# Groups of the last batch in the attention's last steps, and a home of its own for the second MoE's first 512 tokens

## The chip, the core and the metric

The kernel runs on one core of one Trainium2 chip. The metric is the time of one execution on the device in microseconds (us), as the median of the runs shown. An execution under the hardware profiler gave the trace that is read here.

## The reference, cut to what matters

```python
# 4 batches, 8 heads, 576 tokens, head width 64; 2304 tokens in all
q_rot, k_rot = rotate(q), rotate(k)
attn = softmax(q_rot @ k_rot.T / 8); x = (attn @ v) as [2304, 512]
# first MoE: w1, w2, w3 [512, 768], w_out [768, 512]
y = maximum(maximum(x @ w1, x @ w2), x @ w3) @ w_out
# second MoE: w_in [512, 2048], w_out [2048, 512]
h = y @ w_in
out = (h * sigmoid(h)) @ w_out
```

## The kernel before

Every product of float32 accuracy is made of three float16 matmuls on a high and a low part ("split": ScalarE rounds the high part, VectorE takes the rest).

**Attention.** `attention()` runs 80 steps, one tile of 128 query rows each, and four more to drain. A step issues the scores of one tile (`s`, L380 to L390), the maximum of a row on VectorE (`nb`, L400), the exponential on ScalarE (`e`, L407), and for the two tiles before it the division (L419), the transposes on TensorE (`tr`, L434 to L448) with their copies to SBUF (`pt`, L436 to L454), and the product with v (`xp`, L463 and L467) whose result is split into `x` (L470, L471). The attention's PSUM pools stay open until its end.

**First MoE.** `moe1(b, ...)` yields the work of a batch as groups: an "up" group is 12 matmuls on 256 or 320 tokens (`PARTS`: half 0 has 256 tokens, half 1 has 320) for one of the three weights, a "down" group 18. Three up groups make one tile `h`: the first is evacuated by ScalarE (`t`, L560), the second and third by VectorE (`t`, L562). Inside the attention a group has one of the two PSUM buffers `ps_m` (tag `m`); behind the attention `ps_g` (tag `mg`, five buffers) comes to them. In the attention's loop groups of the first three batches are let in by a rate (`RATE`, `debt`); those of the last batch, b = 3, are written behind it. The order within an engine is settled when the program is built, by a scheduler that may move an instruction ahead where its operands allow it.

**Second MoE.** `prep_w7` combines and splits its second weight on POOL (`z`, L793), ScalarE (L797) and VectorE (L801) beside the last batch's groups: eight items, a new one every 5.2 groups, with three buffers `z7`. The first MoE's result lies in DRAM (`yscr`). Nine blocks of 256 tokens follow. Block 0 goes through `s1` in four units (`yt`, L920). Blocks 1 to 8 go in four pairs J = 0 to 3 of 512 tokens through `s1_pair`, eight steps each, which replaces eight products by seven (L952); for that the 512 tokens are loaded into four blocks of a tile `yr` (L742), their largest value is taken over all rows (`y7_max`: L150 on VectorE, then a transpose L117 on TensorE, L119 on VectorE and a broadcast matmul L120), four differences are made on POOL (L987) and the seven forms are split in place (`y7_forms`, L158 and L163): form b overwrites block b from block b + 1. The activations of a unit are combined on POOL (`gsum`, L899), split (L903, L904) and multiplied by `s2` (L1014, L1016). In `s1_pair` VectorE adds the banks `m` and `mb` up (L958), and one of the sums is POOL's (`z`, L966), before ScalarE's activation (L970). `yr` has two buffers of eight blocks; they lie in the space of the first MoE's weights, so that the first load waits for that MoE's last up group. `DIFFS` gives the order of the four differences.

All loads named here go through SyncE's DMA queue (SP), in the order in which they are issued; an issue that waits holds the ones behind it.

```python
DIFFS = ((4, 0, 1), (5, 2, 4), (6, 2, 0), (7, 3, 5))   # out, in0, in1: r[out] = r[in0] - r[in1]
```

Of the kernel before, what the change touches and what calls it, by code (L numbers as in the profile page):

```python
# [17 lines left out]
P = 128  # L18
# [4 lines left out]
def fused_kernel(  # L23
# [52 lines left out]

    left = ExitStack()
    wp1 = Ring(left, "wp1", 1)
    x_p = {0: Ring(left, "x0", 1)}
# [376 lines left out]
    def av(b, hp, r):  # L456
        if hp == 0 and r == 0:
            x_t[b] = x_p[b % 2].tile([P, NP, 2, S], F16, tag="x", name="x")
# [312 lines left out]

    SUMS = ((4, 0, 2, ALU.add), (6, 1, 0, ALU.subtract), (5, 4, 1, ALU.subtract), (7, 3, 5, ALU.subtract))
    DIFFS = ((4, 0, 1), (5, 2, 4), (6, 2, 0), (7, 3, 5))
# [103 lines left out]
    def moe2(st, pools, rings, ps_a, wo_rest, w7, w8_load):  # L877
        z_p, yr_p, ga_p, sum_p, g7_p, tm_p, o_p = pools
# [15 lines left out]
        def g_split(jb, u, g):  # L894
# [3 lines left out]
            for o, x, y, op in SUMS:  # L898
                nc.gpsimd.tensor_tensor(out=q[o], in0=q[x], in1=q[y], op=op)  # L899
# [77 lines left out]
        def y7_max(r):  # L977
            m = small.tile([P, 1], F32, tag="ym", name="ym")
            absmax(m, flat(r[:, 0:4]))
            return m  # L980

        def y7_sums(J, r, m):
            s, sg, ch, co = y_scales(m, 2, st)
            for jb in (1 + 2 * J, 2 + 2 * J):
                sg_t[jb], co_t[jb] = sg, co
            for o, x, y in DIFFS:
                nc.gpsimd.tensor_tensor(out=r[:, o], in0=r[:, x], in1=r[:, y], op=ALU.subtract)  # L987
            return s, ch

        def y7_forms(J, r, s, ch, lo_hi=range(7)):  # L990
            for b in lo_hi:
                t = r[:, b].bitcast(F16)
                split(t[:, 0:512], t[:, 512:1024], r[:, b + 1], s)
            if lo_hi[-1] == 6:
                sc[J] = [r[:, b].bitcast(F16).rearrange("p (x c n) -> p x c n", x=2, c=2) for b in range(7)], ch
# [77 lines left out]
        raw = y7_load(0)  # L1073
        for n in range(UNITS):
# [11 lines left out]
        for J in range(nb // 2):  # L1086
            A, B = 1 + 2 * J, 2 + 2 * J
            more = J + 1 < nb // 2
            for p in range(HB):
# [6 lines left out]
                if p == 2 and more:  # L1096
                    sums = y7_sums(J + 1, raw, m)
                if p > 2 and more:
                    y7_forms(J + 1, raw, *sums, lo_hi=((0,), (1,), (2, 3), (4, 5), (6,))[p - 3])
# [77 lines left out]
    for j, _ in enumerate(attention(), 1):  # L1177
# [35 lines left out]
    def w8_load(k):  # L1213
        t = w8a.tile([P, 2, 2, 7, P], F16, tag="w8s", name="w8s")
        p = k % HB
        if k < HB:
            for c in range(2):
                nc.sync.dma_start(out=t[:, c, :, 0:4], in_=w8scr[:, p, c, :, 0:4])
# [64 lines left out]
```

## Time and profile before

| what | value |
|---|---|
| median of three runs | 1032.52 us (1030.5 to 1036.38) |
| the profiled execution, its own time | 1033.06 us |
| its span in the trace | 1031.3 us |
| TensorE (PE) busy | 957.4 us, 93% of the span |
| VectorE (DVE) busy | 687.4 us, 67% |
| ScalarE (ACT) busy | 617.8 us, 60% |
| GpSimd (POOL) busy | 490.3 us, 48% |
| mean granted clock of TensorE | 0.976 |

The span is what the trace covers; 1.76 us of the execution's own time lie around it. Busy time of an engine is the time in which one of its instructions ran. In a row of the timeline the numbers are start, length, engine, line, operation and operands; brackets give the idle time before it on its engine and what ended it.

### The profile page before, as it was taken

How to read it: one execution, taken by the hardware profiler on the slowest of the kernel's cores; microseconds unless marked ns; L12 is line 12 of the kernel's file. 1: busy time of each engine (PE TensorE's matmuls, PEld its weight loads, DVE VectorE, ACT ScalarE, POOL GpSimd, SP SyncE). 2: the span in 40 equal slices, each digit the busy share in tenths (PEclk: the TensorE clock that was granted, in tenths of full speed). 3: DMA queues.
4: the chain of work that ended last, by engine and by line, in shares of the span. 5: the costliest groups of instructions: out<-in, count | busy, mean ns of one | idle time of the engine just before them, and what ended most of it. 6: DMA issues, size and time to landing. Idle time of an engine off the chain costs nothing.

```text
span 1031.3 us, 19508 instructions
## 1 busy us (share of the span) xinstructions
PE 957.4 (93%) x7234; PEld 716.3 (69%) x7234; DVE 687.4 (67%) x1295; ACT 617.8 (60%) x1377; POOL 490.3 (48%) x548
## 2 busy tenths in 40 slices
PE   4776988999999999989999999998999999999997
PEld 2443665666666766666766668777888888888886
DVE  6669787765577655677576646645678866867454
ACT  3778676656757767768777744534565644644342
POOL 6835593961247601543232205536269457356164
PEclk9688999999999999999999999999999999999999
DMA  6943123512434411544444414254444343342201
GB/s 151 281 117 102 32 75 90 139 51 68 137 97 121 118 47 41 164 140 138 133 134 138 144 61 165 82 186 146 129 151 162 105 154 111 109 129 95 89 3 42
DMA packets 126063, 118.00 MB, mean 114 GB/s; under 512 B 47376, under 2 KB 109584, under 8 KB 125968
## 3 DMA queue, kind: packets, MB, share of 16 engines
q1 hardware_dynamic: 124464, 116.03, 37.6%
q8 instruction: 57, 0.93, 0.4%
q10 hardware_dynamic: 1504, 0.72, 0.3%
q14 instruction: 38, 0.31, 0.1%
HBM read 90.51 MB, written 26.21 MB: 113 GB/s over the span
## 4 chain that ended last, share of the span: by engine, by line
PE 55%; DVE 10%; POOL 7%; ACT 5%; issue 4%; DMA 4%; SPq 1%; DVEq 0%; ACTq 0%; POOLq 0%
PE m L544 15%; PE m L952 5%; PE xp L467 5%; PE tr L448 4%; PE s L390 4%; PE mb L952 4%; POOL gsum L899 4%; PE mg L544 3%; PE c L1016 3%; PE b L1016 2%; PE a L1016 2%; DVE nb L400 2%; POOL yr L987 1%; PE d L1016 1%; DMA yr<-yscr 1%
## 5 line engine op out<-in xcount | busy, mean ns | idle before, releaser
L544 PEld LDWEIGHTS <-w 128*128 128x128 f16 x1632 | 157.8, 98 | 65.3 <-issue 24.6
L544 PE MATMUL m<-x,w 128*128 128x256 f16 (+1 forms) x1336 | 189.8, 287 | 9.6 <-ACT t L560 4.2
L1016 PEld LDWEIGHTS <-g 128*128 128x128 f16 x1485 | 145.2, 98 | 19.5 <-issue 2.3
L952 PEld LDWEIGHTS <-w8s 128*128 128x128 f16 x1344 | 131.0, 98 | 20.6 <-issue 5.3
L400 DVE TENSOR_REDUCE nb<-s 128x2 f32<-128x1152 f32 (+1 forms) x80 | 98.7, 1234 | 48.4 <-PE s L390 39.1
L407 ACT ACTIVATE e<-s,nb 128x576 f32<-128x576 f32 x144 | 105.2, 736 | 41.3 <-DVE nb L400 34.8
L212 POOL TENSOR_SCALAR z<-z 128x256 uint16<-128x256 uint16 x64 | 56.6, 885 | 142.4 <-DVE z L211 128.6
L793 POOL TENSOR_TENSOR z<-z 128x128 f32<-128x128 f32 (+1 forms) x96 | 59.8, 640 | 127.6 <-DMA z<-zwo 37.3
L448 PE MATMUL tr<-ident,e 128*128 128x128 f32 x576 | 98.5, 289 | 16.8 <-ACT T L350 6.1
L419 ACT ACTIVATE e<-e,rec 128x576 f32<-128x576 f32 x144 | 104.4, 767 | 15.3 <-DVE rec L417 14.7
L448 PEld LDWEIGHTS tr<-ident,e 128*128 128x128 f32 x576 | 69.8, 147 | 52.9 <-issue 11.6
L952 PE MATMUL m<-yr,w8s 128*128 128x256 f16 x768 | 90.7, 273 | 4.2 <-DVE t L958 4.2
L467 PE MATMUL xp<-pt,vd 128*64 128x256 f32 (+1 forms) x512 | 83.6, 423 | 0.0
L452 ACT ACTIVATE pt<-tr 128x384 f32<-128x384 f32 x119 | 56.5, 485 | 44.8 <-PE tr L448 44.5
L390 PE MATMUL s<-T 64*128 64x512 f32 x256 | 80.4, 690 | 0.0
L966 POOL TENSOR_TENSOR z<-t 128x256 f32<-128x256 f32 x32 | 27.9, 873 | 94.1 <-DVE t L958 55.9
L952 PE MATMUL mb<-yr,w8s 128*128 128x256 f16 x576 | 69.4, 273 | 2.3 <-ACT yr L158 2.1
L544 PE MATMUL m<-h,wo 128*128 128x256 f16 (+1 forms) x448 | 64.4, 286 | 0.5 <-POOL wo L160 0.5
L904 DVE SCALAR_TENSOR_TENSOR g<-gsum,sg,g 128x1024 f16<-128x1024 f32 x36 | 49.1, 1373 | 22.5 <-ACT g L903 22.0
L544 PEld LDWEIGHTS <-wo 128*128 128x128 f16 x512 | 49.3, 98 | 17.8 <-issue 5.8
L903 ACT ACTIVATE g<-gsum,sg 128x1024 f16<-128x1024 f32 x36 | 40.7, 1141 | 33.2 <-POOL gsum L899 33.2
L467 PEld LDWEIGHTS xp<-pt,vd 128*64 128x64 f32 x512 | 36.7, 138 | 33.4 <-issue 16.0
(231 smaller groups left out, 1919.9 us busy)
## 6 DMA issues: line engine op xcount, KB each, us to landing
w8s<-w8scr SPq DMA_DIRECT2D x64, 448.0 KB, 4.3
z<-in_moe_w_in_dram SPq DMA_DIRECT2D x32, 256.0 KB, 3.1
z<-in_moe_w_out_dram SPq DMA_DIRECT2D x32, 256.0 KB, 3.2
w<-in_moe_w_dram SPq DMA_DIRECT2D x6, 768.0 KB, 5.7
wo<-in_moe_w_dram SPq DMA_DIRECT2D x6, 768.0 KB, 5.6
qk<-in_q_dram SPq DMA_DIRECT2D x32, 128.0 KB, 3.0
vd<-in_v_dram SPq DMA_DIRECT2D x16, 256.0 KB, 3.2
zwi<-z SPq DMA_DIRECT2D x32, 128.0 KB, 3.1
```

The costliest lines, as they stand in the source:

```text
L212: nc.gpsimd.tensor_scalar(out=q[:, :, 2], in0=q[:, :, 1], scalar1=step, scalar2=off, op0=ALU.mult, op1=ALU.add)
L390: last["s"] = nc.tensor.matmul(s[:, o:o + 512], qs[r], kt[r], start=True, stop=True).ins
L400: x = nc.vector.tensor_reduce(out=nb[:, 0:m], in_=both(s, 0, 960, 576) if m > 1 else s[:, 0:576], op=ALU.max, axis=AX.X, negate=True)
L407: x = nc.scalar.activation(out=e[:, HK[g]], in_=s[:, SK[g]], func=AF.Exp, bias=nb[:, g:g + 1], accum_out=sm[:, g:g + 1])
L419: nc.scalar.activation(out=e[:, HK[g]], in_=e[:, HK[g]], func=AF.Copy, scale=r[:, g:g + 1])
L448: nc.tensor.transpose(tr[:, i * n:(i + 1) * n], e[0:n, c * P:(c + 1) * P], ident[0:n, 0:n])
L452: nc.scalar.activation(out=to, in_=of, func=AF.Copy)
L467: nc.tensor.matmul(xp[r, 0:n], v4[:, g, c, :], pt[:, c + 5 * g, :], start=False, stop=(c == 3))
L544: nc.tensor.matmul(ps[:, 0:n], l, r, start=(first and i == 0), stop=(not more and i == len(passes) - 1))
L793: nc.gpsimd.tensor_tensor(out=z[:, o], in0=z[:, x], in1=z[:, y], op=op)
L952: nc.tensor.matmul(o, l, r, start=(i == 0), stop=(i == len(passes) - 1))
L1016: x = nc.tensor.matmul(ps, l, r, start=first, stop=last_, skip_group_check=True)
```

## The change

1. In the attention's last eight steps one group of the last batch's first half is taken per step.
2. The tile of `x_p[0]` (9,216 bytes in a row; the `x` of batches 0 and 2) is allocated outside the first MoE's pools and kept. Even pairs J = 0 and 2 load their four blocks of 512 tokens there (`y7_even`); the four differences go into a tile `ye` of its own. Odd pairs keep `yr`, which now has one buffer.
3. Pair 0 is loaded at group 14 of the last batch's rest, behind the first four loads of `w8s`, and measured at group 15; the measure stood in `s1`'s second unit before. Its differences and first two forms stand ahead of `s1`, the other forms in its first two units.
4. The differences of the later pairs are held behind the last `gsum` that is written before them (`issue_after`). `DIFFS` has its second and third entries exchanged.
5. `prep_w7` starts an item every 4.4 groups, and block 0 is measured at group 9 of the rest in place of 12.

```diff
+    x_p = {0: Ring(ctx, "x0", 1)}
     left = ExitStack()
     wp1 = Ring(left, "wp1", 1)
-    x_p = {0: Ring(left, "x0", 1)}
...
+    def y7_even(J):
+        r = x_p[0].tile([P, NP * S], F32, tag="x", name="x")
+        return y_load(1 + 2 * J, r[:, 0:4 * 512].rearrange("p (a n) -> p a n", a=4), 512), None
+
+    def y7_block(r, o):
+        return r[o // 4][:, o % 4]
...
-    DIFFS = ((4, 0, 1), (5, 2, 4), (6, 2, 0), (7, 3, 5))
+    DIFFS = ((4, 0, 1), (6, 2, 0), (5, 2, 4), (7, 3, 5))
...
+                last["gsum"] = nc.gpsimd.tensor_tensor(out=q[o], in0=q[x], in1=q[y], op=op).ins
...
         def y7_load(J):
-            return y_load(1 + 2 * J, yr_p.tile([P, 8, 512], F32, tag="yr", name="yr"), 512)
...
+            if J % 2 == 0:
+                return y7_even(J)
+            r = yr_p.tile([P, 8, 512], F32, tag="yr", name="yr")
+            return y_load(1 + 2 * J, r[:, 0:4], 512), r[:, 4:8]
...
+            r = r[0], r[1] if J % 2 else ye_p.tile([P, 4, 512], F32, tag="ye", name="ye")
+            with tc.issue_after(last["gsum"]) if J else nullcontext():
+                for o, x, y in DIFFS:
+                    nc.gpsimd.tensor_tensor(out=y7_block(r, o), in0=y7_block(r, x), in1=y7_block(r, y), op=ALU.subtract)
+            return r, s, ch
...
-        raw = y7_load(0)
+        sums = y7_sums(0, st["y7"], st["y7s"])
+        y7_forms(0, *sums, lo_hi=(0, 1))
         for n in range(UNITS):
             s1(n)
             splits()
             rest_step(5)
-            if n == 1:
-                m = y7_max(raw)
+            if n < 2:
+                y7_forms(0, *sums, lo_hi=((2, 3), (4, 5, 6))[n])
             if n == 2:
                 second(0, 0)
-                y7_forms(0, raw, *y7_sums(0, raw, m))
...
+        if nxt[0] == B - 1 and j > len(tiles) - 4 and nxt[1] == 0:
+            nxt = next(moe)
...
-    chain = prep_w7(z7_p, w7_p, w7, 5.2)
+    chain = prep_w7(z7_p, w7_p, w7, 4.4)
...
-        if n == 12:
+        if n == 9:
             st["y0"] = y_split(y0, yt_p, st)
+        if n == 14:
+            with tc.issue_after(last["early"]):
+                st["y7"] = y7_even(0)
+        if n == 15:
+            st["y7s"] = y_scales(y7_max(st["y7"]), 2, st)
```

**How the order moves on TensorE, at the attention's last tile.** A row with `m` or `mg` is one matmul of the first MoE's last batch (12 make a group), `tr` are the attention's transposes, `xp` its product with v. Before:

```order
L448 MATMUL tr_6990<-ident_78,e_6892 128x128 x3
L434 MATMUL tr_6995<-ident_78,e_6923 128x128 x4
L439 MATMUL tr_7002<-ident_78,e_6923 128x128
L440 MATMUL tr_7002<-ident_78,e_6923 64x128
L463 MATMUL xp_7007<-pt_6931,vd_0_129 128x320
L467 MATMUL xp_7007<-pt_6931,vd_0_129 64x320 x8
L544 LDWEIGHTS w_0_138
L544 MATMUL mg_7107<-x_5774,w_0_138 128x256
```

Nothing stands between the last transposes and the last product. The same place in the change, with the repeats of a group's matmuls left out:

```order
L448 MATMUL tr_7053<-ident_78,e_6922 128x128 x3
L544 LDWEIGHTS w_0_138
L544 MATMUL m_7190<-x_5774,w_0_138 128x256
...
L544 MATMUL m_7304<-x_5774,w_0_138 128x256
...
L434 MATMUL tr_7073<-ident_78,e_6971 128x128 x4
L439 MATMUL tr_7080<-ident_78,e_6971 128x128
L440 MATMUL tr_7080<-ident_78,e_6971 64x128
...
L544 MATMUL m_7328<-x_5774,w_0_138 128x256
...
L463 MATMUL xp_7103<-pt_6979,vd_0_129 128x320
L467 MATMUL xp_7103<-pt_6979,vd_0_129 64x320 x8
```

Three groups now lie around the last transposes. From the first group of the last batch to the last `xp` there were 4 groups, and there are 11.

**On POOL, at the second MoE's start.** `yr_7974` is pair 0, `yr_8446` pair 1, the numbers of `gsum` are block 0's units. Before:

```order
L987 TENSOR_TENSOR yr_7974<-yr_7974 128x512 x4
L899 TENSOR_TENSOR gsum_8038<-ga_7979 128x256 x2
L987 TENSOR_TENSOR yr_8446<-yr_8446 128x512 x2
L899 TENSOR_TENSOR gsum_8107<-ga_8048 128x256
L899 TENSOR_TENSOR gsum_8038<-gsum_8038,ga_7979 128x256
L899 TENSOR_TENSOR gsum_8107<-ga_8048 128x256
L987 TENSOR_TENSOR yr_8446<-yr_8446 128x512
```

Eight differences stand among the first units' sums. In the change (`x_7514` is pair 0's new home):

```order
L1003 TENSOR_TENSOR ye_8002<-x_7514 128x512 x2
L1003 TENSOR_TENSOR ye_8002<-x_7514,ye_8002 128x512 x2
L915 TENSOR_TENSOR gsum_8070<-ga_8011 128x256 x2
L915 TENSOR_TENSOR gsum_8070<-gsum_8070,ga_8011 128x256
L915 TENSOR_TENSOR gsum_8070<-ga_8011,gsum_8070 128x256
L915 TENSOR_TENSOR gsum_8144<-ga_8085 128x256 x2
```

Only pair 0's four are left there, ahead of all sums; pair 1's have gone behind the sums of block 1's first unit.

**On POOL, where pair 0's steps end and pair 1's begin.** `yr_9273` is pair 2, `z_2` the sum of L966. Before:

```order
L899 TENSOR_TENSOR gsum_9320<-gsum_9320,z_1_8782 128x256
L987 TENSOR_TENSOR yr_9273<-yr_9273 128x512
L899 TENSOR_TENSOR gsum_9320<-z_1_8782,gsum_9320 128x256
L987 TENSOR_TENSOR yr_9273<-yr_9273 128x512
L899 TENSOR_TENSOR gsum_9200<-z_0_8384 128x256 x2
L987 TENSOR_TENSOR yr_9273<-yr_9273 128x512
L899 TENSOR_TENSOR gsum_9200<-gsum_9200,z_0_8384 128x256
L966 TENSOR_TENSOR z_2_9211<-t_1_9261 128x2x128
L987 TENSOR_TENSOR yr_9273<-yr_9273 128x512
```

Three differences stand ahead of `z_2`. In the change:

```order
L915 TENSOR_TENSOR gsum_9203<-gsum_9203,z_0_8387 128x256
L915 TENSOR_TENSOR gsum_9203<-z_0_8387,gsum_9203 128x256
L982 TENSOR_TENSOR z_2_9214<-t_1_9264 128x2x128
L915 TENSOR_TENSOR gsum_9456<-z_1_8785 128x256 x2
L915 TENSOR_TENSOR gsum_9456<-gsum_9456,z_1_8785 128x256
L1049 TENSOR_TENSOR ob_9335<-t_0_9336 128x256
L915 TENSOR_TENSOR gsum_9456<-z_1_8785,gsum_9456 128x256
L1003 TENSOR_TENSOR ye_9548<-x_9276 128x512 x2
```

All four stand behind `z_2` and two units' sums. The same exchange is found between pairs 1 and 2.

## Rows read from the trace of the kernel before

**Rows 1.** The page, part 1: busy time, share of the span, instructions.
```profile
PE 957.4 (93%) x7234; PEld 716.3 (69%) x7234; DVE 687.4 (67%) x1295; ACT 617.8 (60%) x1377; POOL 490.3 (48%) x548
```
**Rows 2.** Busy time by stretch: PE, PEld, DVE, ACT, POOL; granted clock, DMA share, GB/s.
```profile
582.79:613.77 30.98, 28.36 (x175) 17.15 (x175) 15.08 (x40) 19.57 (x51) 1.79 (x4) 0.94 0.20 65
613.77:680.87 67.10, 65.93 (x533) 51.98 (x532) 41.08 (x64) 28.47 (x48) 29.70 (x32) 1.00 0.35 111
680.87:720.00 39.13, 35.64 (x318) 30.63 (x316) 19.45 (x25) 18.36 (x23) 25.85 (x24) 1.00 0.67 219
775.00:810.00 35.00, 32.67 (x296) 28.47 (x294) 27.97 (x46) 17.70 (x27) 26.58 (x26) 1.00 0.40 130
860.00:885.00 25.00, 22.50 (x204) 19.58 (x202) 16.44 (x33) 12.23 (x19) 16.27 (x19) 1.00 0.41 122
```
**Rows 3.** PE's waits from 582.79 to 613.77: total us, times, longest.
```profile
PE xp L463 <- DVE pt L442: 1.0, 1, 1.0
PE tr L448 <- ACT pt L452: 0.7, 2, 0.5
PE tr L434 <- ACT e L419: 0.6, 1, 0.6
PE tr L448 <- DVE pt L442: 0.4, 1, 0.4
```
**Rows 4.** PE's timeline, two products of 16 matmuls; PE busy and granted clock between.
```profile
572.56 2.37 PE L467 MATMUL xp<-pt,vd 128*64 128x320 f32 x16
610.03 3.81 PE L467 MATMUL xp<-pt,vd 128*64 128x320 f32 x16
...
611.00:612.00 1.00, 1.00 (x6) 0.50 0.00 0
```
**Rows 5.** PE's timeline, a run of up groups; PE's waits in the whole program.
```profile
619.57 6.17 PE L544 MATMUL mg<-x,w 128*128 128x256 f16 x55
...
PE m L544 <- DVE t L562: 6.7, 6, 1.9
PE m L544 <- ACT t L560: 4.2, 2, 3.1
```
**Rows 6.** PE's waits from 560 to 780, those behind the attention.
```profile
PE mb L952 <- ACT yr L158: 2.1, 1, 2.1
PE m L120 <- DVE amax L119: 1.2, 1, 1.2
...
PE m L920 <- DMA w8s<-w8scr: 0.9, 1, 0.9
```
**Rows 7.** Timeline of SP's DMA queue.
```profile
619.04 20.90 SPq L850 DMA_DIRECT2D z<-zwo  x10
...
681.29 1.46 SPq L742 DMA_DIRECT2D yr<-yscr  x3
...
686.64 6.26 SPq L1218 DMA_DIRECT2D w8s<-w8scr  x8
```
**Rows 8.** POOL's timeline, pair 0's first difference; all L987, ns min/median/max.
```profile
686.60 1.27 POOL L987 TENSOR_TENSOR yr<-yr 128x512 f32<-128x512 f32 x1 [21.57 <-DMA yr<-yscr]
...
L987 POOL TENSOR_TENSOR yr<-yr x16: 1251/1268/2082, 686.6 to 862.2; 128x512 f32<-128x512 f32 x16
```
**Rows 9.** Timelines of POOL, ACT and PE where pair 1 begins.
```profile
786.73 1.27 POOL L987 TENSOR_TENSOR yr<-yr 128x512 f32<-128x512 f32 x1
...
789.58 0.72 ACT L970 ACTIVATE z<-z,ch 128x512 f32<-128x512 f32 x1 [1.97 <-POOL z L966]
...
796.72 2.78 PE L952 MATMUL m<-yr,w8s 128*128 128x256 f16 x24 [1.41 <-DVE t L958]
```
**Rows 10.** Timelines of POOL, ACT and PE where pair 2 begins.
```profile
854.13 2.50 POOL L987 TENSOR_TENSOR yr<-yr 128x512 f32<-128x512 f32 x2 [4.58 <-DMA yr<-yscr]
...
864.80 0.72 ACT L970 ACTIVATE z<-z,ch 128x512 f32<-128x512 f32 x1 [3.91 <-POOL z L966]
...
873.52 2.78 PE L952 MATMUL m<-yr,w8s 128*128 128x256 f16 x24 [2.23 <-DVE t L958]
```

More of the change, by code (lines that the diff above doesn't have):

```diff
@@ L770, in y_split, with y7_max, y7_form @@
         return yt, sg, ch, co
+    def y7_even(J):
+        r = x_p[0].tile([P, NP * S], F32, tag="x", name="x")
+        return y_load(1 + 2 * J, r[:, 0:4 * 512].rearrange("p (a n) -> p a n", a=4), 512), None
+    def y7_max(r):
+        m = small.tile([P, 1], F32, tag="ym", name="ym")
+        absmax(m, flat(r[0]))
+        return m
+    def y7_block(r, o):
+        return r[o // 4][:, o % 4]
+    def y7_form(r, b, s):
+        t = y7_block(r, b).bitcast(F16)
+        split(t[:, 0:512], t[:, 512:1024], y7_block(r, b + 1), s)
     SUMS = ((4, 0, 2, ALU.add), (6, 1, 0, ALU.subtract), (5, 4, 1, ALU.subtract), (7, 3, 5, ALU.subtract))
-    DIFFS = ((4, 0, 1), (5, 2, 4), (6, 2, 0), (7, 3, 5))
+    DIFFS = ((4, 0, 1), (6, 2, 0), (5, 2, 4), (7, 3, 5))
     HB = NF2 // 2
@@ L877, in moe2 @@
     def moe2(st, pools, rings, ps_a, wo_rest, w7, w8_load):
-        z_p, yr_p, ga_p, sum_p, g7_p, tm_p, o_p = pools
+        z_p, yr_p, ye_p, ga_p, sum_p, g7_p, tm_p, o_p = pools
         co_t, g7, acc, sc, gB, gA, ready = {0: st["y0"][3]}, {}, {}, {}, {}, {}, {}
@@ L974, in y7_load, with y7_sums @@
         def y7_load(J):
-            return y_load(1 + 2 * J, yr_p.tile([P, 8, 512], F32, tag="yr", name="yr"), 512)
[L977 to L983, printed above, removed]
+            if J % 2 == 0:
+                return y7_even(J)
+            r = yr_p.tile([P, 8, 512], F32, tag="yr", name="yr")
+            return y_load(1 + 2 * J, r[:, 0:4], 512), r[:, 4:8]
+        def y7_sums(J, r, scales):
+            s, sg, ch, co = scales
             for jb in (1 + 2 * J, 2 + 2 * J):
                 sg_t[jb], co_t[jb] = sg, co
-            for o, x, y in DIFFS:
-                nc.gpsimd.tensor_tensor(out=r[:, o], in0=r[:, x], in1=r[:, y], op=ALU.subtract)
-            return s, ch
+            r = r[0], r[1] if J % 2 else ye_p.tile([P, 4, 512], F32, tag="ye", name="ye")
[3 more added lines that the diff above has]
+            return r, s, ch
         def y7_forms(J, r, s, ch, lo_hi=range(7)):
             for b in lo_hi:
-                t = r[:, b].bitcast(F16)
-                split(t[:, 0:512], t[:, 512:1024], r[:, b + 1], s)
+                y7_form(r, b, s)
             if lo_hi[-1] == 6:
-                sc[J] = [r[:, b].bitcast(F16).rearrange("p (x c n) -> p x c n", x=2, c=2) for b in range(7)], ch
+                sc[J] = [y7_block(r, b).bitcast(F16).rearrange("p (x c n) -> p x c n", x=2, c=2) for b in range(7)], ch
         def s2(jb, u):
@@ L1096, in moe2 @@
                 if p == 2 and more:
-                    sums = y7_sums(J + 1, raw, m)
+                    sums = y7_sums(J + 1, raw, y_scales(m, 2, st))
                 if p > 2 and more:
-                    y7_forms(J + 1, raw, *sums, lo_hi=((0,), (1,), (2, 3), (4, 5), (6,))[p - 3])
+                    y7_forms(J + 1, *sums, lo_hi=((0,), (1,), (2, 3), (4, 5), (6,))[p - 3])
                 if p == 5:
@@ L1217, in w8_load @@
             for c in range(2):
-                nc.sync.dma_start(out=t[:, c, :, 0:4], in_=w8scr[:, p, c, :, 0:4])
+                last["early"] = nc.sync.dma_start(out=t[:, c, :, 0:4], in_=w8scr[:, p, c, :, 0:4]).ins
         else:
@@ L1236, in fused_kernel @@
         Ring(ctx, nm, bufs)
-        for nm, bufs in (("yr_p", 2), ("ga_p", 3), ("sum_p", 2), ("g7_p", 3), ("tm_p", 2), ("o_p", 1))
+        for nm, bufs in (("yr_p", 1), ("ye_p", 1), ("ga_p", 3), ("sum_p", 2), ("g7_p", 3), ("tm_p", 2), ("o_p", 1))
     )
```

3 lines of the change are left out of this document (1 added, 2 removed).

## The prediction

> **What bounds the kernel now.** I read the page's table of engines first, then the busy time by stretch, then the waits in each stretch that the change touches, and last the timelines around the longest waits. The table shows TensorE busy for 93% of the span [rows 1], and no other engine above 67%, so a microsecond is to be had where TensorE stands still or runs slowly, and nowhere else. The stretches show where that is [rows 2]: busy time taken from length gives 30.98 - 28.36 = 2.62 us of idle time in the attention's last steps, 67.10 - 65.93 = 1.17 in the rest of the last batch, 39.13 - 35.64 = 3.49 at the second MoE's start, 35.00 - 32.67 = 2.33 where pair 1 begins and 25.00 - 22.50 = 2.50 where pair 2 begins. That is 12.1 us. To it comes a stretch at half clock: the same 16 matmuls of `xp` took 2.37 us at 572 and 3.81 at 610, where the granted clock was 0.50, which is the level of 1.2 GHz; TensorE had just stood waiting for the attention's last copies [rows 3, 4]. That is 1.44 us more. Everything that the change moves lies in these five places, and the matmuls themselves stay as they are, so about 13.6 us bound the gain from above.
>
> **Part 1, the groups in the attention's last steps.** By the order of the instructions TensorE now has 11 groups ahead of the attention's last `xp` where it had 4, so seven groups move ahead. A group of 12 costs 12 x 6.17 / 55 = 1.35 us [rows 5], seven cost 9.4 us, and they cost it in either place. What they bring is cover. Each of the waits at 582 to 614 is for a copy or a division that the attention's own chain is late with [rows 3], and at most of these places the new order has a group or more between the transpose and the matmul that waited. I take 2.2 of the 2.62 us. The clock fell behind those waits, and with TensorE busy through them I take all of the clock's loss, 1.4 us; if a gap stays, it is 0. The unknown is what seven more groups do to the two buffers `m`: a group can't start before the one two places ahead of it has been evacuated, and its evacuation stands in the queues of ScalarE and VectorE among the attention's exponentials and maxima. The nearest rows are the waits for such evacuations in the whole program, eight of them, 10.9 us together, the longest 3.1 us [rows 5]. So the bounds are a gain of 2.62 and, with the longest of these waits at every one of the seven, a loss of 21.7; the order places the evacuations close behind their groups, so I stay near the upper end, and the 0.4 us that I left out stand for the buffers. VectorE and ScalarE are busy for 15.1 and 19.6 of these 31 us [rows 2], so they have room.
>
> What is late next: the attention ends 9.4 - 2.2 - 1.4 = 5.8 us later, and with it the loads of `w8s`, of `yscr` and of `z`, which wait for its space. The rest of the last batch starts later by the same and is 9.4 us shorter, so from the attention's end to the second MoE there are 67.1 - 9.4 = 57.7 us. POOL's 29.7, ScalarE's 28.5 and VectorE's 41.1 us of work in that stretch [rows 2] fit, though VectorE also gets pair 0's maximum and first forms. The step of 4.4 in place of 5.2 groups makes `prep_w7` end 7 x 0.8 = 5.6 groups sooner, some 7.6 us, which is about what the shorter stretch asks for. I cost it at nothing; its cover is the idle time of POOL ahead of the second MoE, 21.57 us [rows 8].
>
> **Part 2, the measure of block 0 and of pair 0.** Before, TensorE waited 1.17 us for `amax` of block 0 [rows 6]; VectorE had been held up by a split of `w7` whose load was late. In the new order this `amax` stands ahead of those splits, and 24 matmuls on 320 tokens lie between its transpose and its broadcast. A second measure, pair 0's, comes into this stretch. At its old place it cost TensorE no wait, and 33 matmuls lie around it now. Bounds: both wait as the one did (a loss of 1.2) or neither (a gain of 1.17). I take 0.8.
>
> **Part 3, pair 0 at the second MoE's start.** Its loads stood behind the last stores of the first MoE in the queue (681.29), and ahead of the next `w8s` (686.64) [rows 7]; POOL idled until they came [rows 8]; then its eight differences of 1.27 us shared POOL with the units' sums, and the forms came so late that TensorE waited 2.1 us for ScalarE's, after 0.9 us for `w8s` [rows 6]. Now the four loads go out right behind the first two tiles of `z` (619.04, 5.3 us behind the attention's end), in a stretch in which SP spends 20.90 us on ten issues, most of it waiting for buffers [rows 7], and need no space of the first MoE's weights. The differences wait only for the last up group's space and run in POOL's idle time, 4 x 1.27 = 5.1 of 21.57 us. Two of the forms stand ahead of the first activation on ScalarE: if the differences were late, they would hold it, but the idle time is four times their length. On SP the next `w8s` have four loads ahead of them in place of eight. I take 2.7 of the 3.49 us; the bounds are 0 (the forms are late again) and 3.49.
>
> **Part 4, the differences of later pairs.** Where pair 1 begins, POOL ran three differences of pair 2 ahead of `z`; ScalarE, which works in order, waited 1.97 us for `z` and only then split the next `gsum`, VectorE's additions came behind that, and TensorE waited 1.41 us for a bank [rows 9]. Where pair 2 begins it is the same with pair 3: ScalarE waited 3.91, TensorE 2.23 us [rows 10]. The new order puts all of the differences behind `z` and the sums in question. Three of them are 3.8 us, more than either wait, so these 3.64 us should go. The remaining 4.83 - 3.64 = 1.19 us hang on VectorE's maximum of 2,048 columns and on `amax`, which stay. I take 3.4. Pair 1's differences (5.1 us) now stand ahead of `z` at about 740, a new place. The bounds are the whole 4.83, and a loss of 2.23, the longest wait of this kind, should it come back there.
>
> **A rule that speaks against part 4.** A difference took 1,268 ns in the median and 2,082 at most [rows 8]. The Trainium skill, SBUF: State Buffer, "Who interferes with whom", says that a VectorE instruction with two SBUF inputs and a GpSimd instruction that reads SBUF hold each other up entirely. The spread of these durations agrees with it. By that rule moved differences are dear wherever VectorE adds and splits; this is the second rival below.
>
> **The sum.** 2.2 + 1.4 + 0.8 + 2.7 + 3.4 = 10.5 us. The profiled execution took 1033.06 us, which gives 1022.6; it stood 0.5 us above the median of 1032.52, so I forecast a median of 1022.5 us, a gain of 1.0%. A difference of 0.5%, here 5.2 us, is about what a measurement of this kernel can tell from none, so faster means below 1027.4 and slower above 1037.7.
>
> **The rivals.**
> - *The wait moves to the second MoE.* The attention ends 5.8 us later, and what begins there (loads of `z`, POOL's `prep_w7`, pair 0's differences behind it, the forms) comes late in a stretch shortened to 57.7 us. Against it: POOL's 21.57 us of idle time. For it: before, POOL worked in three bursts with gaps for loads, so that not its busy time but the round of three buffers may set the end, which a smaller step can't shorten. Then parts 2 and 3 bring nothing: 1022.5 + 0.8 + 2.7 = 1026.0 us. Chance 0.15.
> - *POOL's differences cost the same at their new places.* If each took its longest time, 2.08 for 1.27 us, beside VectorE's additions, the twelve that are moved behind sums would take 9.7 us more of POOL, and a wait of the old kind would come up behind them. Part 4 then brings nothing (1025.9), and with one new wait of 2.23 us at pair 1's differences 1028.1. Chance 0.13.
> - *The two buffers `m` hold the attention up* (slower). In the last eight steps each group must be evacuated in time by an engine that works in order through the attention. If each of the seven waits w, the gain is 10.5 - 7w: nothing at 1.5 us each, a loss of over 0.5% from 2.2 us each, which lies below the longest wait of 3.1 us [rows 5]; at 3.1 us the time is 1022.5 + 21.7 = 1044.2 us. For it: the groups come closer together than anywhere earlier in the attention. Against it: the eight waits of the whole program come to 10.9 us, 1.4 us each, and VectorE is idle for half of that stretch. Chance 0.05.
>
> **How the numbers follow.** The forecast has the rest, 0.67. Its own range goes from all of the idle and slow time gone, 1033.06 - 13.55 - 0.5 = 1019.0, to two thirds of the sum, 1025.5. The first two rivals reach 1028.1. With the run to run spread of the median the range is 1018.5 to 1028.5; the third rival and the tails stay outside, some 0.12. Faster: nearly all of the forecast's 0.67, 0.10 of the first rival's and 0.05 of the second's, 0.81. Same: the rest of those two and a little of the other, 0.14. Slower: 0.05.
>
> **What would show it.** Part 1: the four waits for `pt` and `e` [rows 3] gone, the granted clock at 1.00 at the last `xp`, whose 16 matmuls take 2.4 us, and no new waits of L544 for `t`. Part 2: no wait of L120. Part 3: `ye` computed ahead of the first `gsum`, and no wait of L952 for a form or of L920 for `w8s`. Part 4: no wait of L952 for `t` where pairs 1 and 2 begin, and none new at 740. The prediction is wrong if TensorE's idle time from 582 to 885 stays above 7 us, or if the granted clock falls at another place that the groups have left behind.

## The result, and the profile after

| | before | changed |
|---|---|---|
| median | 1031.08 us (five runs, 1030.5 to 1036.38) | 1020.71 us (five runs, 1020.31 to 1023.01) |
| ratio | | 0.9886, 95% interval 0.9862 to 0.991 |
| profiled execution, span | 1033.06, 1031.3 us | 1020.64, 1018.9 us |

The change is faster by 1.1%, and the measured time lies 1.8 us under the forecast of 1022.5 us and inside its range. Two more runs of the kernel before stand beside the three that the forecast started from, hence its other median. The page of the changed kernel, its table of engines:

```profile
PE 954.2 (94%) x7234; PEld 717.2 (70%) x7234; DVE 689.7 (68%) x1295; ACT 617.6 (61%) x1377; POOL 494.7 (49%) x548
```

Against [rows 1] the share of TensorE grew by one point, because the span shrank: its work is the same. So the time must have come out of its idle and slow stretches. To see that cleanly, equal work is compared: from the product `xp` of the attention's fourth tile from the end to the end of the last matmul. What stands ahead of it is the same in all kernels of this study, instruction by instruction on TensorE, VectorE, ScalarE and POOL. The stretch holds 3,841 matmul records in each, and I split it at the second MoE's first matmul. The busy time by stretch of the kernel before (columns: stretch, length, busy time of PE and its records, granted clock, DMA share, GB/s):

```profile
571.92:680.87 108.95, 105.14 (x781) 0.98 0.32 102
680.87:1025.94 345.07, 336.75 (x3062) 1.00 0.37 119
571.92:1025.94 454.02, 441.89 (x3841) 1.00 0.36 115
```

The same of the changed kernel:

```profile
571.73:673.93 102.20, 102.20 (x784) 1.00 0.37 119
673.93:1013.62 339.69, 336.62 (x3059) 0.99 0.37 118
571.73:1013.62 441.89, 438.82 (x3841) 1.00 0.37 118
```

The stretch is 12.13 us shorter, which is the difference of the two spans (12.4) but for 0.3 us. Of it 6.75 us come from ahead of the second MoE (three small matmuls of pair 0's measure now stand there too) and 5.38 from the second MoE. Idle time fell from 12.13 to 3.07 us (that the gain in length is 12.13 us too is chance). Busy time fell by 3.07 us as well, though the work is the same; the last section says why. What is left stands in one place. By tens of microseconds:

```profile
770.00:780.00 10.00, 9.67 (x90) 1.00 0.29 96
780.00:790.00 10.00, 9.91 (x92) 1.00 0.50 154
790.00:800.00 10.00, 7.35 (x51) 0.83 0.22 81
800.00:810.00 10.00, 10.00 (x95) 1.00 0.28 92
```

All windows from 560 to 770 and from 800 to 1010 read 10.00 at a clock of 1.00. The waits of TensorE from 575 us on are these two (total, times, longest):

```profile
PE m L117 <- DVE t L974: 2.6, 1, 2.6
PE m L968 <- DVE t L974: 0.3, 1, 0.3
```

None of [rows 3] is left, and of [rows 6] neither the form, nor `amax`, nor `w8s`. The waits of [rows 9, 10] are gone where pair 2 begins; where pair 1 begins a longer one has come. (Lines moved: L952 is now L968, L958 is L974, L966 is L982, L987 is L1003, L904 is L920.) Its chain reads so in the timeline (start, length, engine, line, operands, count, idle time before it and what ended it):

```profile
780.88 3.71 POOL L1003 TENSOR_TENSOR ye<-x 128x512 f32<-128x512 f32 x2
784.56 1.25 POOL L1003 TENSOR_TENSOR ye<-x,ye 128x512 f32<-128x512 f32 x1
785.78 0.72 POOL L982 TENSOR_TENSOR z<-t 128x256 f32<-128x256 f32 x1
...
787.84 1.26 POOL L1003 TENSOR_TENSOR ye<-x,ye 128x512 f32<-128x512 f32 x1
...
780.26 1.74 DVE L920 SCALAR_TENSOR_TENSOR g<-gsum,sg,g 128x1024 f16<-128x1024 f32 x1
...
788.11 1.80 DVE L920 SCALAR_TENSOR_TENSOR g<-z,sg,g 128x768 f16<-128x768 f32 x1 [3.99 <-ACT g L919]
789.84 1.74 DVE L920 SCALAR_TENSOR_TENSOR g<-gsum,sg,g 128x1024 f16<-128x1024 f32 x1
...
783.83 0.72 ACT L986 ACTIVATE ga<-ga,ch 128x512 f32<-128x512 f32 x1 [4.33 <-DVE ga L974]
786.53 0.72 ACT L986 ACTIVATE z<-z,ch 128x512 f32<-128x512 f32 x1 [1.98 <-POOL z L982]
...
789.16 1.04 PE L1031 MATMUL a<-w,g 128*128 128x256 f16 x8
792.85 0.27 PE L117 MATMUL m<-ident,ym 128*1 128x128 f32 x1 [2.65 <-DVE t L974]
792.96 0.81 PE L1031 MATMUL a<-w,g 128*128 128x256 f16 x4
793.56 2.77 PE L1031 MATMUL c<-w,g 128*128 128x256 f16 x12
```

It is the chain of [rows 9, 10] one step further on: three differences of pair 2 stand on POOL ahead of a step's `z`, ScalarE waits 1.98 us for that `z` and only then does the splits behind it, VectorE stands idle for 3.99 us, and its additions, which give the banks `m` back, end late. The next matmul that needs a bank happens to be the measure's transpose, L117. Behind the stop 12 matmuls of `c` take 2.77 us, at half clock; at the full clock 12 take 1.47.

### The profile page after: what moved, and what is told of

Its sections match the earlier page's. It is cut to its first block, busy times and chain, and to the rows that moved or that the text cites. A ratio compares the mean times of both kernels' runs of the same rounds, so it can differ in the third digit from the quotient of the medians.

```text
span 1018.9 us, 19509 instructions
## 1 busy us (share of the span) xinstructions
PE 954.2 (94%) x7234; PEld 717.2 (70%) x7234; DVE 689.7 (68%) x1295; ACT 617.6 (61%) x1377; POOL 494.7 (49%) x548
## 4 chain that ended last, share of the span: by engine, by line
PE 67%; DVE 8%; ACT 4%; POOL 3%; issue 2%; DMA 1%; SPq 0%; DVEq 0%; ACTq 0%; POOLq 0%
PE m L544 16%; PE m L968 7%; PE mb L968 6%; PE xp L467 5%; PE tr L448 4%; PE mg L544 4%; PE s L390 4%; PE c L1031 4%; PE a L1031 4%; PE b L1031 4%; PE d L1031 2%; DVE nb L400 2%; POOL gsum L915 1%; PE mb L936 1%; PE m L936 1%
## 5 line engine op out<-in xcount | busy, mean ns | idle before, releaser
L544 PE MATMUL m<-x,w 128*128 128x256 f16 (+1 forms) x1388 | 195.6, 286 | 9.8 <-ACT t L560 4.0
L544 PEld LDWEIGHTS <-w 128*128 128x128 f16 x1632 | 157.7, 98 | 65.3 <-issue 24.1
L968 PEld LDWEIGHTS <-w8s 128*128 128x128 f16 x1344 | 131.1, 98 | 16.1 <-issue 0.9
L407 ACT ACTIVATE e<-s,nb 128x576 f32<-128x576 f32 x144 | 105.4, 737 | 42.5 <-DVE nb L400 35.9
L982 POOL TENSOR_TENSOR z<-t 128x256 f32<-128x256 f32 x32 | 27.0, 845 | 89.1 <-DVE t L974 54.0
L544 PE MATMUL m<-h,wo 128*128 128x256 f16 (+1 forms) x448 | 64.4, 286 | 0.5 <-POOL wo L160 0.5
L920 DVE SCALAR_TENSOR_TENSOR g<-gsum,sg,g 128x1024 f16<-128x1024 f32 x36 | 49.1, 1372 | 22.0 <-ACT g L919 21.6
L544 PEld LDWEIGHTS <-wo 128*128 128x128 f16 x512 | 49.3, 98 | 17.8 <-issue 5.8
L330 POOL TENSOR_TENSOR w<-qk,sin_sb 128x384 f32<-128x384 f32 (+1 forms) x44 | 45.5, 1054 | 26.2 <-DMA qk<-in_q_dram 17.9
L562 DVE SCALAR_TENSOR_TENSOR t<-m,t 128x256 f32<-128x256 f32 (+1 forms) x82 | 37.0, 451 | 20.0 <-PE m L544 16.2
```

What stands on the lines that cost most here:

```text
L407: x = nc.scalar.activation(out=e[:, HK[g]], in_=s[:, SK[g]], func=AF.Exp, bias=nb[:, g:g + 1], accum_out=sm[:, g:g + 1])
L544: nc.tensor.matmul(ps[:, 0:n], l, r, start=(first and i == 0), stop=(not more and i == len(passes) - 1))
L968: nc.tensor.matmul(o, l, r, start=(i == 0), stop=(i == len(passes) - 1))
```

## The experiments

In the table are all kernels: where the equal stretch begins in the trace, its length, TensorE's busy and idle time in it, the number of its stops (idle times of 0.01 us or more), how often in it the granted clock fell to 0.50, and the ratio of the runs to those of the kernel before that were taken with them, with its interval.

| kernel | begins | length | busy | idle | stops | falls | median | ratio |
|---|---|---|---|---|---|---|---|---|
| before | 571.92 | 454.02 | 441.89 | 12.13 | 17 | 1 | 1031.08 | |
| the change | 571.73 | 441.89 | 438.82 | 3.07 | 3 | 1 | 1020.71 | 0.9886 (0.9862 to 0.991) |
| groups alone | 572.72 | 447.36 | 440.29 | 7.07 | 10 | 1 | 1026.97 | 0.995 (0.993 to 0.997) |
| without the groups | 570.43 | 448.32 | 442.20 | 6.12 | 10 | 2 | 1026.33 | 0.9941 (0.992 to 0.9962) |
| without the rule for differences | 574.19 | 446.09 | 439.36 | 6.73 | 6 | 1 | 1024.48 | 0.9929 (0.9904 to 0.9954) |
| differences behind z | 570.99 | 437.87 | 437.16 | 0.71 | 3 | 0 | 1017.84 | 0.9868 (0.9838 to 0.9899) |
| the change again | 570.60 | 442.42 | 439.08 | 3.34 | 4 | 1 | 1020.99 | 0.9882 (0.9851 to 0.9912) |
| differences behind z again | 571.78 | 437.88 | 437.15 | 0.73 | 3 | 0 | 1018.16 | 0.9852 (0.9826 to 0.9878) |
| rule for pair 1 alone | 573.44 | 441.05 | 437.47 | 3.58 | 5 | 0 | 1022.02 | 0.9891 (0.9868 to 0.9914) |
| four groups | 571.15 | 446.45 | 440.45 | 6.00 | 11 | 1 | 1025.48 | 0.9924 (0.9899 to 0.995) |
| early load, late measure | 569.44 | 442.20 | 437.76 | 4.44 | 5 | 0 | 1020.98 | 0.9895 (0.9874 to 0.9916) |
| late load | 571.07 | 445.88 | 439.34 | 6.54 | 7 | 1 | 1024.16 | 0.9919 (0.9896 to 0.9941) |

No edit changes the instructions ahead of the stretch, yet it begins anywhere between 569.44 and 574.19 us. So nearly 5 us of the spread between these executions arise ahead of what is studied here, and where a few microseconds are to be told apart, the length of the stretch says more than the median.

**Groups alone.** The kernel before, with

```diff
+        if nxt[0] == B - 1 and j > len(tiles) - 4 and nxt[1] == 0:
+            nxt = next(moe)
-    chain = prep_w7(z7_p, w7_p, w7, 5.2)
+    chain = prep_w7(z7_p, w7_p, w7, 4.4)
-        if n == 12:
+        if n == 9:
```

> The kernel before with the eight groups alone (the step of 4.4 and block 0's measure at its new place go with them; pair 0 stays as it was). Theory: the attention's last steps bring about 6.0 us by themselves, as in the trace of the change, and block 0's measure some 0.7, so 1024.4 us (ratio 0.9935), with the last 16 matmuls of xp at 2.4 us and TensorE busy throughout 583 to 616. By the prediction's sum, 3.6 + 0.8: 1026.7 us (0.9957). Rival, the wait moves to the second MoE's start: TensorE's idle time there grows from 3.5 to over 7 us because pair 0 is now late by what the attention's end is late, and 1028.5 us or more comes out (0.9975).

The stretch became 454.02 - 447.36 = 6.66 us shorter, the theory's size, with no stop left ahead of the second MoE. Ahead of it 7.19 us were gained; behind it 0.53 were lost again. The interval of the ratio holds both sums and leaves out the rival's 0.9975. At the second MoE's start the waits stayed:

```profile
PE mb L952 <- ACT yr L158: 2.1, 1, 2.1
...
PE m L920 <- DMA w8s<-w8scr: 0.4, 1, 0.4
```

They are no longer than before, where they were 2.1 and 0.9 us. So the attention may end later by the groups' time without the next stage waiting longer for it. The 0.53 us come from the clock, which fell behind the wait of 2.1 us here (0.83 from 710 to 720 us) and hadn't in the kernel before; shorter waits in the second MoE, 7.07 us for 8.32, give the rest back.

**Without the groups.** The change, with the first edit above undone, the step at 5.2 and the measures at groups 17, 22 and 23.

> The change without the eight groups (step 5.2 again, the measures at the same distance from the last batch's end). Theory: parts 2, 3 and 4 bring what the change's trace shows behind the attention, 0.7 + 5.0 + 0.4 = 6.1 us, so 1025.0 us (ratio 0.9941); the attention's last steps idle for 2.6 us and the last xp runs at half clock as before. By the prediction's sum, 0.8 + 2.7 + 3.4 = 6.9: 1024.2 us (0.9933), with no wait where pairs 1 and 2 begin. Rival, pair 0's early load pays only because the groups made room: 1028 us or more, with over 2 us of waits at the second MoE's start.

5.70 us: near the theory's 6.1. The second MoE's start has no wait, with or without the groups, so pair 0's home pays by itself. The two halves add up to 6.66 + 5.70 = 12.36 us against 12.13 together, but that is in part luck: their idle times fell by 5.06 and 6.01 us, 11.07 in all, against 9.06 together, and one more fall of the clock (near 800 us, besides the old one near 607) takes about as much back.

**Without the rule for the differences.**

```diff
-            with tc.issue_after(last["gsum"]) if J else nullcontext():
+            if True:
```

> The change without the rule that puts the later pairs' differences behind the sums. Theory: that rule removed one wait and made another of the same length (2.65 us and a slow clock where pair 1 begins), so its net is 0.4 us: 1021.1 us (1.000 of the change), with the waits where pairs begin at other places but 2 to 5 us in all. By the prediction's sum it is worth 3.4 us: 1024.1 us (1.0033 of the change). Rival, the rule itself costs: 1018 us or less.

The stretch grew by 4.20 us. My theory's 1.000 is wrong, and the prediction's price of 3.4 us looks right, but not for its reason. The largest wait is a new one, in the second MoE's first units:

```profile
681.97 1.27 POOL L1003 TENSOR_TENSOR yr<-yr 128x512 f32<-128x512 f32 x1 [1.61 <-DMA yr<-yscr]
...
684.87 2.95 POOL L1003 TENSOR_TENSOR yr<-yr 128x512 f32<-128x512 f32 x2
687.79 2.57 POOL L915 TENSOR_TENSOR gsum<-ga 128x256 f32<-128x256 f32 x2
690.32 1.27 POOL L1003 TENSOR_TENSOR yr<-yr 128x512 f32<-128x512 f32 x1
...
695.97 1.15 ACT L919 ACTIVATE g<-gsum,sg 128x1024 f16<-128x1024 f32 x1 [2.50 <-POOL gsum L915]
...
697.17 0.28 PE L1029 MATMUL b<-w,g 128*128 128x256 f16 x1 [3.15 <-ACT g L919]
```

Without the rule the scheduler puts pair 1's differences (`yr`) ahead of and between the first sums of block 0, since nothing else holds them there; the sums come late, ScalarE's split too, and TensorE stops for 3.15 us. This run therefore mixes two places, and the run with the rule for pair 1 alone takes them apart.

**The differences behind z.** TensorE's order stays the same, and on POOL the later pairs' differences move behind the `z` of the pair's third step. On VectorE and ScalarE a few instructions change places with a neighbour, none of them from 741 to 799 us, where the wait stood:

```diff
-            nc.gpsimd.tensor_tensor(out=place(gb, 0), ...)
+            last["z"] = nc.gpsimd.tensor_tensor(out=place(gb, 0), ...).ins
-            with tc.issue_after(last["gsum"]) if J else nullcontext():
+            with tc.issue_after(last["z"]) if J else nullcontext():
```

> The change with the later pairs' differences put behind POOL's z of the pair's third step instead of behind the last gsum; TensorE's order is the same, POOL's alone moves. Theory: the wait of 2.65 us where pair 1 begins comes from three differences (5.0 us) that stand ahead of z on POOL; behind z they hold nobody, the wait and the slow clock behind it go, 2.65 + 1.3 us: 1016.8 us (0.9962 of the change), TensorE busy for over 9.9 of every 10 us from 770 to 1000. Rival 1, differences cost the same wherever they stand, since they and VectorE's splits hold each other up: a wait of 2 us or more comes up at the next z or the next forms, 1020.7 us. Rival 2, the wait is the measure's, which takes a bank m between two groups: the same wait of 2.6 us stays at the same place, 1020.7 us.

As the theory said: 4.02 us less than the change, and 0.71 us of idle time in 437.87. The same place in its timeline:

```profile
782.56 0.77 POOL L982 TENSOR_TENSOR z<-t 128x256 f32<-128x256 f32 x1 [2.35 <-DVE t L974]
...
789.76 0.78 POOL L982 TENSOR_TENSOR z<-t 128x256 f32<-128x256 f32 x1 [2.35 <-DVE t L974]
790.50 2.49 POOL L1003 TENSOR_TENSOR ye<-x 128x512 f32<-128x512 f32 x2
792.95 3.34 POOL L1003 TENSOR_TENSOR ye<-x,ye 128x512 f32<-128x512 f32 x2
...
788.45 1.04 PE L1031 MATMUL a<-w,g 128*128 128x256 f16 x8
789.76 0.27 PE L117 MATMUL m<-ident,ym 128*1 128x128 f32 x1 [0.27 <-DVE t L974]
...
790.30 1.47 PE L1031 MATMUL c<-w,g 128*128 128x256 f16 x12
```

`z` now runs as soon as VectorE has made its operand, the differences fill the time to the next `z` at 799.51, and nobody waits for them. Both rivals fall: the measure's transpose stands where it stood and waits 0.27 us, and the differences, 5.83 us for four, are no cheaper than before, but hold nobody.

**The change and this version on one chip.** Both kernels unchanged, in the next two runs.

> The change as it is, beside the next three on one chip. Both theories: a ratio of 0.9886 to the kernel before, and in its profile 0.3 + 2.65 us of idle time between 770 and 800 with a slow clock behind it.

> The differences behind z once more, on the chip of the change. Theory (they hold nobody there): 4.0 us under the change, ratio to before 0.985, TensorE's idle time from the attention's last steps to the end 0.7 us. Rival (the gap between them on two chips was chance): the same time as the change.

The stretch is 442.42 - 437.88 = 4.54 us shorter, the median 2.83 us. The two intervals of the ratios (0.9851 to 0.9912, 0.9826 to 0.9878) overlap, but both carry the spread of the kernel before. Directly, ten of the change's eleven runs took 1019.8 us or more, and ten of this version's eleven 1019.59 or less; the traces agree, in both pairs. At 1.3% and 1.5% under the kernel before, this is the best version of the study.

**The rule for pair 1 alone.**

```diff
-            with tc.issue_after(last["gsum"]) if J else nullcontext():
+            with tc.issue_after(last["gsum"]) if J == 1 else nullcontext():
```

> The change with the rule kept for pair 1's differences alone; those of pairs 2 and 3 go back to where they were before, ahead of z and between the sums. It tells the two things apart that the run without the rule mixed. Theory: at pairs 2 and 3 the rule removed 3.6 us of idle time and brought 3.1 with a slow clock of 1.2, so without it there nothing is gained or lost: 1020.0 us (1.000 of the change; 0.9880 to before), with the old waits of 0.6, 1.4, 0.4 and 0.9 us where pairs 1 and 2 begin and none at 695 us. By the prediction's sum, 3.4 us of loss, all of it at pairs 2 and 3: 1024 us. Rival, the waits at 695 us had another cause than the order of pair 1's differences: they stay, 1024 us too but with 3 us idle at 695.

The old waits are back, the one where pair 2 begins with 0.93 us for the 2.23 of before, and the new one at 695 us is not:

```profile
PE m L968 <- DVE t L974: 2.9, 3, 1.4
PE m L117 <- DVE t L974: 0.6, 2, 0.4
```

The stretch is 441.05 us, 0.84 us shorter than the change's and 1.37 shorter than its second run's. So at pairs 2 and 3 the rule brought nothing in these executions; with it there are 3.07 us of idle time and a slow clock, without it 3.58 and none. The median of 1022.02 us lies between the 1020.0 and the 1024 that were expected and decides nothing. Even without the rule the five waits are 1.25 us shorter than before; whether the exchange in `DIFFS` or the new homes did that was not taken apart. The 446.09 - 441.05 = 5.04 us that it is worth lie at pair 1's differences, where the kernel before had no loss to remove.

**Four groups** in place of eight, with the measures and the step moved in proportion:

```diff
-        if nxt[0] == B - 1 and j > len(tiles) - 4 and nxt[1] == 0:
+        if nxt[0] == B - 1 and j > len(tiles) and nxt[1] == 0:
```

> The change with four groups let into the attention's last steps in place of eight (step 4.8 and the measures at the same distance from the last batch's end). Theory: each wait of the last steps is covered by the group that stands at its place, so those whose place is filled go and the others stay; the longest, 0.97 us ahead of the last xp, and the half clock behind it go with the last groups: 1 to 2 us over the change, 1022 us. Rival, cover is needed only at the end and eight are no better than four: the same time as the change. Rival 2, the two buffers m were a price that eight pay and four don't: under the change by up to 1 us.

4.56 us over the change, two to four times what I expected. Two of the five waits are gone, those of 0.23 and 0.58 us ahead of the last transposes, where two more groups stand now. Those of 0.46, 0.37 and 0.97 us stay, at places without a group, and two came, ahead of the first group that moved: 0.18 us for a weight's maximum (L120) and 0.36 for an exponential (L407). That leaves 2.35 us of 2.62, and `amax` of block 0 costs 0.50 us again. The half clock at the last `xp` is gone:

```profile
594.05 0.38 PE L120 MATMUL m<-amax,ones 1*128 1x1 f32 x2 [0.18 <-DVE amax L119]
594.78 0.49 PE L387 MATMUL s<-kd,T 128*128 128x128 f32 x2 [0.36 <-ACT e L407]
...
604.72 1.80 PE L544 MATMUL m<-x,w 128*128 128x256 f16 x15
...
607.02 1.47 PE L544 MATMUL m<-x,w 128*128 128x256 f16 x12
...
610.12 0.81 PE L463 MATMUL xp<-pt,vd 128*128 128x320 f32 x2 [0.97 <-DVE pt L442]
610.86 2.37 PE L467 MATMUL xp<-pt,vd 128*64 128x320 f32 x16
```

The stop of 0.97 us ahead of it is the same as in [rows 3]; in that kernel the clock fell behind it, here not. That cover works place by place holds. That the wait of 0.97 us goes with the last groups does not: it stayed. The two new waits do not come from the groups, as far as the trace shows: ScalarE stood idle for 1.95 us, up to 588.36, until a load of `z` for a weight of the second MoE had landed, and what stands behind it on ScalarE and VectorE came late. In the kernel before and in the change the same split had no idle time ahead of it; in the run without the groups it had 1.30 us. The two waits and the price of two stops are about 1 of the 4.56 us. The price on the buffers `m` doesn't show.

**Pair 0 loaded early, measured late.** The change, with measure, differences and forms where they were before:

```diff
-        if n == 15:
-            st["y7s"] = y_scales(y7_max(st["y7"]), 2, st)
...
+            if n == 1:
+                m = y7_max(st["y7"])
             if n == 2:
                 second(0, 0)
+                y7_forms(0, *y7_sums(0, st["y7"], y_scales(m, 2, st)))
```

> The change with pair 0 loaded early as now, but measured, its differences and forms put back into the second MoE's first three units as before. Theory A, the load was what came late: with it early TensorE waits for neither a form nor w8s, and the time is the change's, 1020.9 us (ratio to before 0.988). Theory B, what came late were the measure and the eleven splits and differences behind it, which stand among the units' sums: the wait for the forms stays, 1.5 to 2.5 us at some 712 us, perhaps with a slow clock, so 1023.5 us (0.9908).

442.20 us, the change's length within 0.3, as theory A says, and no wait for a form comes back. But there are two stops more, of 0.64 and 0.52 us at 729 and 736, and the one at 774 is 0.2 us longer; with what a stop costs besides (last section) that is 1.8 us, which the clock pays back here, since it stayed up behind the stop that ends at 792.5. So, by subtraction, the early load is most of part 3, and the early measure some 1.8 us of it.

**Pair 0 loaded late.** The change, with the load behind the first MoE's last store and the measure at once behind it:

```diff
-        if n == 14:
-            with tc.issue_after(last["early"]):
-                st["y7"] = y7_even(0)
...
+        with tc.issue_after(last["ys"]):
+            st["y7"] = y7_even(0)
+        st["y7s"] = y_scales(y7_max(st["y7"]), 2, st)
```

> The change with pair 0 in its home of its own, but loaded only behind the first MoE's last store, where its loads stood before, and measured at once. Theory A: the late load brings the old loss back, 0.9 us for w8s behind the four loads and 2 us for the forms, with five stops in place of none, 4.0 us in all: 1025 us (ratio to before 0.9922). Rival: four loads are half of the eight of before and the home frees POOL of the wait for the space, so that only 1 to 1.5 us comes back, 1022.2 us (0.9895). In both the measure's amax at 680 us, now late, costs a wait of up to 1.2 us more.

3.99 us over the change: theory A's size, though spread otherwise than it said. The two longest of the waits that came to those of the change:

```profile
PE m L936 <- DMA w8s<-w8scr: 2.4, 1, 2.4
PE b L1031 <- ACT g L919: 0.7, 1, 0.7
```

No wait for a form: four differences behind four loads are made in time. The late measure costs 0.25 us (L936 waits for pair 0's scale at 692). The scheduler moved TensorE's work too: the third unit's matmuls stand ahead of half of the second's, and so want their `w8s` sooner, 9.1 us behind the second MoE's first matmul in place of 10.5 in the change:

```profile
675.65 2.18 SPq L742 DMA_DIRECT2D x<-yscr  x4
...
678.66 1.92 SPq L1238 DMA_DIRECT2D w8s<-w8scr  x4
...
681.42 0.39 PE L1031 MATMUL b<-w,g 128*128 128x256 f16 x2 [0.66 <-ACT g L919]
684.17 0.82 PE L936 MATMUL m<-yt,w8s 128*128 128x256 f16 x3 [2.36 <-DMA w8s<-w8scr]
```

The second MoE's first matmul starts at 672.74 here. The first of these `w8s` is issued 5.9 us behind it and lands 11.4 us behind it; in the change, without the four loads ahead of it, these are 5.2 and 8.1 us. So the load comes 3.3 us later, 0.7 from its issue and 2.6 on its way. Had it landed as in the change, there would be no wait in this order either; had TensorE kept the change's order, the wait would be 11.4 - 10.5 = 0.9 us (an estimate), which is theory A's price for `w8s`. The other 1.4 us come from the order of the units. The clock fell behind this wait and not, as in the change, behind the one near 795 us, so it cost no more than there.

## Why the prediction was right, step by step

The sum was 10.5 us, the trace gives 12.4 between the spans and 12.1 in the stretch, the medians 10.4. Two of its terms were too small and one too large, so that the total comes near is luck in part: parts 1 to 3 gave some 4.5 us more than their 7.1, part 4 some 2.9 less than its 3.4. From the sum to the forecast there is a slip as well: 1032.52 - 10.5 is 1022.0, not 1022.5.

In what follows a stop is priced at 0.22 us beside its idle time and a fall of the clock at 1.7 us; both are estimates from the table, worked out in the last section.

**Part 1 and part 2: 3.6 + 0.8 = 4.4 us predicted, 6.75 found, and some 7.0 without the three matmuls of pair 0's measure that came here.** The mechanism is right: all waits of [rows 3] are gone, the 16 matmuls of the last `xp` take 2.37 us as [rows 4] had them at full clock, no new wait of L544 for `t` has come, and of `amax`'s 1.17 us nothing is left (0.29 in the change's second run). The mis-sized terms are the 2.2 us of idle time (the trace: all 2.62), the 0.8 (all 1.17) and the clock's 1.4. The clock had slowed the two matmuls L463 ahead of the 16 as well, 1.01 us for 0.70, so it cost 1.75. That makes 5.5. The rest is the price of the stops themselves: seven at 0.22 us are 1.5, and 7.1 are reached.

**Part 3: 2.7 us predicted, about 4.6 found.** All 3.49 us of idle time went where I took 2.7, and five stops of 0.22 us with them. By the run that measures late, some 1.8 us of it hang on the measure's place, the rest on the load's.

**Part 4: 3.4 us predicted, about 0.5 found; this is the step that failed.** "The new order puts all of the differences behind `z` and the sums in question" holds for the first step of a pair, not for the one in which the differences now stand: there they stand ahead of the next step's `z`. The trace has 4.83 us of idle time in five stops before, 5.9 with the stops' own price, and 3.06 in three after, 3.7 with it, and behind the longest some 1.7 us lost to the half clock. The wait was moved to the next step, not removed, and the clock fell on it. Of the second MoE's 5.38 us these two parts place 5.1, and 0.3 are the measure that left it. It is a wait of the kind that the second rival named, at one of three places: 2.23 us were looked for at pair 1's differences, where none came, and 2.65 came at pair 2's. The prediction also named a fall of the clock at a new place as a sign of being wrong, if the groups left it behind. The clock did fall, at 793 us, but behind this wait, which stands in the run without the groups too. The run behind `z` is what the prediction's sentence promised: it brings the other 4.02 us.

**The rivals.** The wait did not move to the second MoE's start (no wait there). The two buffers `m` did not hold the attention up; with TensorE busy from 571.73 to 673.93 without a stop there is nothing left that they could cost. The upper bound of 13.6 us for the gain was too low: the version behind `z` gains 454.02 - 437.87 = 16.15 us, because the bound counted idle time and one slow stretch, and not what each stop costs besides: 14 stops fewer at 0.22 us are 3.1.

**The rule on VectorE and POOL.** Before, I weighed the second rival by the rule of the Trainium skill, SBUF — State Buffer, "Who interferes with whom". In the changed kernel two differences took 3.71 us beside VectorE's split of 1,024 columns that had started before them, where the same pair takes 2.49 in the version behind `z`: 1.2 us, and they lie on the chain that ends in the wait of 2.65. That much agrees with the rule. By the rule alone, though, differences would be as dear wherever VectorE splits; behind `z` the four took 5.83 us, in the change 3.71 + 1.25 + 1.26 = 6.22, hardly more, and the wait is there in the one and not in the other. Where they stand decides, not what they cost.

## What to carry to other kernels

- When helper work is moved on an in-order engine, name the instruction of the critical chain that comes behind it at the new place, not only the one that it got out of the way of. Here `z` of the next step was that instruction, and one reference to another predecessor brought 4 us.
- Cover from other work counts place by place. A wait goes when a filler stands between its two ends. Half of the fillers took two of five waits, 0.8 of 2.6 us; all of them took everything.
- Compare equal work between two events that both traces have, and split length into busy and idle time. The executions profiled here differ by nearly 5 us before the part that is studied begins.

## What the runs showed of the hardware

**A stop costs more than its idle time.** The profile gives the last matmul of a run its full length, so that the end of it counts as busy. In the changed kernel:

```profile
702.10 1.47 PE L1031 MATMUL c<-w,g 128*128 128x256 f16 x12
703.41 0.82 PE L1031 MATMUL d<-w,g 128*128 128x256 f16 x6
704.06 0.82 PE L968 MATMUL m<-x,w8s 128*128 128x256 f16 x6
```

Six more matmuls take 0.65 us, 0.108 each, and each of these groups has 0.17 us more than that; the next group starts 0.16 or 0.17 us before the end of the one ahead. In a running stream the end lies under the next matmul; at a stop it doesn't, and the time is lost though it reads as busy. The single matmul of 0.27 us, against the spacing of 0.108, is the same thing. The Trainium skill, TensorE: Matmul & The Clock Gate, "Single matmul latency", has the length of a single matmul as its columns plus a fixed 398, in cycles of the full clock, which gives an estimate of 0.272 us for 256 columns; the trace's 0.27 agrees, though the profile models where a matmul ends.

The table gives the price of a stop a second time. If its twelve busy times are fitted by a constant, a price for each stop and a price for each fall of the clock, they come out as 436.5 us, 0.22 and 1.7 (an estimate), and no kernel is off by more than 0.33 us. Between the kernel before and the version behind `z` there are 14 stops and one fall less, 3.0 + 1.7 = 4.7 of the 4.73 us by which busy time differs; between it and the change there are 14 stops less and as many falls, 3.0 of 3.07 us. The records show 0.16 of the 0.22 us; where the rest of it lies stays open.

**Whether the clock falls behind a stop isn't told by the stop's length.** The stop of some 2.65 us near 790 stands in six executions. In four of them (the change, its second run, without the groups, four groups) the clock fell: the ten microseconds from 790 on read 0.83, 0.83, 0.93 (and 0.90 in the next ten) and 0.84. In the two with pair 0 measured or loaded late it did not. The window of the run with the early load and late measure:

```profile
790.00:800.00 10.00, 7.46 (x67) 1.00 0.18 64
```

Against the change's 7.35 and 0.83 above, this is the same stop with the clock kept at its level of 2.4 GHz. The busy time of the whole stretch is 437.76 us in place of 438.82, although that run has two stops more. Behind a stop of 2.14 us the clock fell in the run with the groups alone and not in the kernel before. With the late load it fell behind the stop of 2.36 us near 682 instead. And in the kernel before it had fallen behind a stop of only 0.97 us, which had two more, of 0.23 and 0.58, just ahead of it [rows 3, 4]. What decides it stays open here; a forecast should carry such a fall as a chance, at some 1.7 us.
